# Both half pairs of the first group by halves, with plain fp32 value products for the whole group, in an attention and gated convolution kernel

## The chip, the cores and the metric

One core of one Trainium2 chip runs the whole program. The engines are named as the profile names them: PE (TensorE matmuls), PEld (its weight loads), DVE (VectorE), ACT (ScalarE), POOL (GpSimd) and SP, which here only issues the DMAs. The metric is the device time of one execution in microseconds, lower is better, as the median of repeated executions.

## The reference

Attention within chunks of 64 positions, then a block that gates a projection with a short causal convolution, over 8 batches of 576 positions, 8 heads of 64:

```python
scores = scale * np.matmul(q_c, k_c.transpose(0, 1, 2, 4, 3))      # per chunk of 64 x 64
scores = scores - np.max(scores, axis=-1, keepdims=True)
attn = np.exp(scores)
attn = attn / (np.sum(attn, axis=-1, keepdims=True) + 1e-09)
out = np.matmul(attn, v_c)
# x: (8, 576, 512), the heads side by side
for k in range(5):
    gate_pre += conv_w[k][None, None, :] * xp[:, k:k + S, :]
gate = 1.0 / (1.0 + np.exp(-gate_pre))
val = x @ w_val
return gate * val @ w_out
```

## The kernel before

The 4608 positions are cut into nine groups `g` of 512. In a group the eight heads are two half pairs `p`, and each half pair has two halves `b` of eight blocks of 64 x 64 scores. The channels of x are four chunks `c` of 128, two for each half pair (`c = 2p` and `2p + 1`). All work is written as small pieces, and the string `ORDER` is the program: it lists the pieces one after another, and every engine runs its instructions in the order in which the pieces stand there. `SLOTS` gives each new tile its buffer, in the same order. Nothing is rearranged later, and the waits between engines follow from which piece reads what. All instructions are recorded under one line (L160, the helper `run`), so the rows are read by their tiles.

The pieces of one half pair, in the order in which they need each other: `lq`, `lk`, `lv` (loads of 512 KB), `S g p b` (PE: 16 matmuls 64 x 64, two records each, for one half), `mx` (DVE: row maximum), `sb` (DVE: subtract it), `ex` (ACT: exp), `sm` (DVE: row sum and reciprocal), `nm` (POOL, or `nmD` on DVE: divide), `T` (PE: eight transposes), `ec` (ACT: copy of the transposes out of PSUM), `A` (PE: probabilities times v, giving x), `xc` (ACT: copy of x). `ey` is another way for `sb`, `ex` and `sm`, with a bias and an accumulated sum on ACT.

For the value projection there are two forms. `V g m c` makes three fp32r products for output chunk m and input chunk c (weights v_hi, v_lo, v_hi; x as a rounded part `xr` and a rest `xd`). `F 0 m c` makes one plain fp32 product from the weights before their split (`wq`) and the copied x; the trace records it as two matmuls. The weights arrive as 64 bit numbers, and the pieces `w1` to `w7` put each of the four chunks `v 0` to `v 3` into fp32, on POOL (with a G), DVE and ACT; `w6` and `wb` then split it into v_hi and v_lo.

The other pieces are `k0`, `k` (convolution taps, DVE), `sg` (gate), `gs`, `gr`, `gd` (gate times value, split in two), `P` (output projection, three fp32r products each), `oc`, `st` (copy and store). `W n` makes n matmuls of a zero tile, which nothing reads.

The first group before the change: its two half pairs have one `mx`, `sb`, `ex`, `sm`, `nm`, `T`, `ec`, `A` each, over all sixteen blocks. For half pair (0, 1) the maximum is subtracted by four matmuls on PE (`mh`, `ml`, `sp`, `ep`). `F` serves the chunks c = 0 and 1, `V` the chunks 2 and 3. The opening holds 22 filler matmuls: `W 2` ahead of the first scores, `W 15` after them, then `W 4` and `W 1`.

The set `BY_HALF` names the half pairs that are worked by halves. It is read in `sc`, `half_scores`, `xc`, `x_part`, `xr` and `xd`; before the change it is empty. For a half pair in it, the scores of its second half go to the PSUM tile `et`, and the pieces take a third number, the half.

Of the kernel before, what the change touches and what calls it, by code (L numbers as in the profile page):

```python
# [626 lines left out]
```

## Time and profile before

| | us |
|---|---|
| median of 3 runs | 282.15 (282.10 to 282.59) |
| the profiled execution | 282.13 |
| its span in the trace | 280.3 |
| PE busy in the span | 268.4 |
| DVE busy | 229.7 |
| ACT busy | 208.4 |
| POOL busy | 131.2 |

The span runs from the first to the last instruction of the core; 1.8 us of the execution's own time lie around it. A record of a matmul begins when it starts to stream and ends with its modelled end, so records overlap, and the step from one start to the next tells what one costs.

### The profile page before, as it was taken

How to read it: one execution, taken by the hardware profiler on the slowest of the kernel's cores; microseconds unless marked ns; L12 is line 12 of the kernel's file. 1: busy time of each engine (PE TensorE's matmuls, PEld its weight loads, DVE VectorE, ACT ScalarE, POOL GpSimd, SP SyncE). 2: the span in 40 equal slices, each digit the busy share in tenths (PEclk: the TensorE clock that was granted, in tenths of full speed). 3: DMA queues.
4: the chain of work that ended last, by engine and by line, in shares of the span. 5: the costliest groups of instructions: out<-in, count | busy, mean ns of one | idle time of the engine just before them, and what ended most of it. 6: DMA issues, size and time to landing. Idle time of an engine off the chain costs nothing.

```text
span 280.3 us, 7931 instructions
## 1 busy us (share of the span) xinstructions
PE 268.4 (96%) x3330; PEld 214.4 (76%) x3330; DVE 229.7 (82%) x316; ACT 208.4 (74%) x472; POOL 131.2 (47%) x109
## 2 busy tenths in 40 slices
PE   3979999989999999999999999999999999999994
PEld 2456787867888877888788888888888778888883
DVE  0899999999989999999979998899999676691200
ACT  2477999999899979768796968999687767324331
POOL 1857935093104243991584007379212748642510
PEclk9999999999999999999999999999999999999999
DMA  7999958456002735076442034961104001000526
GB/s 276 417 409 375 322 196 341 125 200 208 0 2 76 268 150 165 24 265 219 160 137 93 1 118 160 317 184 54 40 0 151 4 2 75 0 0 2 187 87 249
DMA packets 14291, 42.47 MB, mean 151 GB/s; under 512 B 1712, under 2 KB 1712, under 8 KB 14256
## 3 DMA queue, kind: packets, MB, share of 16 engines
q1 hardware_dynamic: 14256, 41.97, 41.6%
q8 instruction: 26, 0.43, 0.6%
q14 instruction: 9, 0.07, 0.1%
HBM read 32.53 MB, written 9.44 MB: 150 GB/s over the span
## 4 chain that ended last, share of the span: by engine, by line
PE 89%; DMA 4%; DVE 3%; ACT 1%; issue 1%; POOL 1%; SPq 0%; POOLq 0%
PE ps L160 77%; PE s L160 6%; PE et L160 5%; DMA ld<-in_v 2%; DMA ld<-in_q 1%; DVE rs L160 1%; DVE t L160 1%; DVE mx L160 1%; POOL t L160 1%; ACT t L160 1%; DVE e_row L160 0%; ACT e_row L160 0%; SPq L160 0%; ACT x L160 0%; DVE ml L160 0%
## 5 line engine op out<-in xcount | busy, mean ns | idle before, releaser
L160 DVE SCALAR_TENSOR_TENSOR acc<-x,cw,acc 128x516 f32<-128x516 f32 (+1 forms) x144 | 109.6, 799 | 4.1 <-ACT acc L160 2.3
L160 PE MATMUL ps<-t,v_hi 128*128 128x512 f32 x232 | 81.6, 403 | 0.0
L160 PEld LDWEIGHTS ps<-t,v_hi 128*128 128x128 f32 x232 | 43.6, 188 | 10.5 <-issue 0.5
L160 PE MATMUL ps<-t,v_lo 128*128 128x512 f32 x112 | 44.3, 396 | 0.0
L160 PE MATMUL ps<-o_hi,t 128*128 128x512 f32 x92 | 34.5, 397 | 0.0
L160 DVE TENSOR_REDUCE mx<-s 128x16 f32<-128x1024 f32 x18 | 21.7, 1207 | 7.1 <-PE s L160 7.1
L160 DVE TENSOR_TENSOR t<-ps,t 128x512 fp32r<-128x512 f32 (+1 forms) x27 | 18.0, 683 | 11.1 <-PE ps L160 4.7
L160 PEld LDWEIGHTS s<-ld,ld 64*64 64x64 f32 x1152 | 19.7, 139 | 9.1 <-issue 9.1
L160 PE MATMUL s<-ld,ld 64*64 64x64 f32 x1152 | 22.0, 225 | 4.8 <-DMA ld<-in_q 3.3
L160 PEld LDWEIGHTS ps<-t,v_lo 128*128 128x128 f32 x112 | 21.1, 188 | 5.1 <-issue 0.5
L160 POOL TENSOR_TENSOR t<-e_row,rs 128x1024 f32<-128x1024 f32 x11 | 22.3, 2030 | 1.8 <-DVE cw_h L160 1.1
L160 ACT COPY x<-ps 128x512 f32<-128x512 f32 (+3 forms) x46 | 20.8, 499 | 1.2 <-PE ps L160 1.0
L160 ACT ACTIVATE acc<-x,cw 128x516 f32<-128x516 f32 (+1 forms) x28 | 20.9, 746 | 0.1
L160 PEld LDWEIGHTS ps<-o_hi,t 128*128 128x128 f32 x92 | 17.3, 188 | 4.2
L160 ACT ACTIVATE e_row<-s,mx 128x64 f32<-128x64 f32 x64 | 19.2, 348 | 0.0
L160 PE MATMUL ps<-o_lo,t 128*128 128x512 f32 x48 | 18.9, 394 | 0.0
L160 ACT ACT_TABLE_LOAD x14 | 18.0, 1283 | 1.0 <-PEq L616 0.7
L160 ACT CAST t<-ps 128x512 fp32r<-128x512 f32 x28 | 16.3, 604 | 3.0 <-PE ps L160 3.0
L160 DVE TENSOR_REDUCE rs<-e_row 128x16 f32<-128x1040 f32 x14 | 17.2, 1229 | 0.5 <-ACT e_row L160 0.5
L160 PEld LDWEIGHTS et<-ident,t 128*128 128x128 f32 x128 | 14.6, 141 | 4.0 <-issue 2.1
L160 PE MATMUL et<-ident,t 128*128 128x128 f32 x128 | 16.8, 274 | 0.3 <-DVE t L160 0.3
L160 ACT ACTIVATE e_row<-e_row 128x1024 f32<-128x1024 f32 x13 | 13.9, 1066 | 4.0 <-DVE e_row L160 4.0
(303 smaller groups left out, 609.3 us busy)
## 6 DMA issues: line engine op xcount, KB each, us to landing
ld<-in_k SPq DMA_DIRECT2D x18, 512.0 KB, 5.1
ld<-in_q SPq DMA_DIRECT2D x18, 512.0 KB, 5.9
ld<-in_v SPq DMA_DIRECT2D x18, 512.0 KB, 5.0
out<-t SPq DMA_DIRECT2D x10, 256.0 KB, 4.5
acc<-in_moe_w_val SPq DMA_DIRECT2D x4, 512.0 KB, 7.7
acc<-in_moe_w_out SPq DMA_DIRECT2D x4, 512.0 KB, 5.3
out<-t2h SPq DMA_DIRECT2D x3, 256.0 KB, 2.5
out<-t2g SPq DMA_DIRECT2D x3, 256.0 KB, 2.7
```

The lines of the kernel that those rows point to most:

```text
L160: return tc.keep_in_program_order(fn(*args, **kwargs))
```

## The change

`BY_HALF` holds both half pairs of the first group. Their scores, maxima, exponentials, sums, divisions, transposes, products with v and copies of x are now pieces for one half of eight blocks each (`mx 0 0 0`, `T 0 1 1` and so on). One half of a half pair gives one whole chunk of x (`xc 0 p u` writes chunk `2p + u`). The four maximum matmuls, and `mh`, `ml`, `sp`, `ep`, are not used any more. All sixteen value products of group 0 are `F`; the eight `V 0` pieces (24 fp32r matmuls) and the `xr` and `xd` of half pair (0, 1) are gone. The fillers are four `W 1`. The rest of `ORDER` and `SLOTS` is a new table for the whole program, with some pieces on other engines.

```diff
-ORDER = """zw,zi,zr 0,zr 1,lk 0 0,lq 0 0,W 2,lw v 2,lw v 0,S 0 0 0,zm,S 0 0 1,mx 0 0,w1 v 2,w5 v 2,sb 0 0,lk 0 1,w3G v 2,w2 v 2,
...
+ORDER = """zw,zi,zr 0,zr 1,lk 0 0,lq 0 0,zm,lw v 1,w3G v 1,S 0 0 0,mx 0 0 0,sb 0 0 0,w1G v 1,ex 0 0 0,S 0 0 1,w5 v 1,mx 0 0 1,
+sb 0 0 1,lk 0 1,ex 0 0 1,sm 0 0 0,nmD 0 0 0,T 0 0 0,W 1,lw v 0,w5 v 0,w2 v 1,w1G v 0,lw v 3,w3G v 3,w2 v 0,lv 0 0,
...
 SLOTS = dict(
...
-    et="000000000000000000",
...
+    et="0000000000000000000000",
...
-    mh="0",
-    ml="0",
 )
...
-BY_HALF = set()
+BY_HALF = {(0, 1), (0, 0)}
```

PE, from its first scores on, before (s and et are the scores and transposes, ld a load, ps a product in PSUM, t a probability or weight tile, x the copied x; the fillers between are left out):

```order
L160 MATMUL s_89<-ld_78,ld_80 64x64 x32
...
L160 MATMUL s_167<-ld_130,ld_138 64x64 x32
...
L160 MATMUL et_222<-ident,t_220 128x128 x8
L160 MATMUL s_233<-ld_218,ld_231 64x64 x32
L160 MATMUL ps_287<-t_267,ld_271 64x64
...
L160 MATMUL ps_335<-x_321,t_136 128x512
```

The same place now, up to the scores of the second group's first half pair (s_267):

```order
L158 MATMUL s_87<-ld_78,ld_80 64x64 x16
L158 MATMUL et_110<-ld_78,ld_80 64x64 x16
L158 MATMUL ps_139<-ident,t_137 128x128 x4
...
L158 MATMUL et_164<-t_162,ld_158 64x64 x16
...
L158 MATMUL ps_188<-ident,t_137 128x128 x4
L158 MATMUL s_198<-ld_131,ld_196 64x64 x16
L158 MATMUL et_224<-t_162,ld_158 64x64 x16
L158 MATMUL ps_245<-x_185,t_183 128x512
L158 MATMUL et_247<-ld_131,ld_196 64x64 x16
L158 MATMUL s_267<-ld_222,ld_217 64x64 x32
```

The first value product (ps_335 before, ps_245 now) stood behind three whole sets of scores; it now stands behind three halves, and behind the transposes and products with v of only one half pair.

DVE in the opening, before:

```order
L160 TENSOR_REDUCE mx_123<-s_89 128x16
L160 TENSOR_SCALAR t_125<-acc_85 128x512
L160 TENSOR_TENSOR e_row_64<-s_89,mx_123 128x16x64
L160 SCALAR_TENSOR_TENSOR t_132<-t_125,t_132 128x512
L160 TENSOR_REDUCE rs_141<-e_row_64 128x16
L160 RECIPROCAL rs_141<-rs_141 128x16
L160 TENSOR_REDUCE mx_200<-s_167 128x16
```

DVE in the opening, now:

```order
L158 TENSOR_REDUCE mx_104<-s_87 128x2x4
L158 TENSOR_TENSOR e_row_64<-s_87,mx_104 128x2x4x64
L158 TENSOR_REDUCE mx_104<-et_110 128x2x4
L158 TENSOR_TENSOR e_row_64<-et_110,mx_104 128x2x4x64
L158 TENSOR_REDUCE rs_134<-e_row_64 128x2x4
L158 RECIPROCAL rs_134<-rs_134 128x2x4
L158 TENSOR_TENSOR t_137<-e_row_64,rs_134 128x2x256
```

The weight pieces (t_125, t_132) that stood between maximum and sum have left this stretch, and the division of the first half (t_137) now comes ahead of the second half's sum.

PE at the later value products of group 0, before (v_hi and v_lo are the split weights) and, in the second fence, now:

```order
L160 MATMUL ps_335<-x_321,t_269 128x512
L160 MATMUL ps_357<-x_321,t_269 128x512
L160 MATMUL et_456<-ident,t_445 128x128 x8
L160 MATMUL s_484<-ld_441,ld_452 64x64 x32
L160 MATMUL ps_357<-t_439,v_hi 128x512
L160 MATMUL ps_357<-t_439,v_lo 128x512
L160 MATMUL ps_357<-t_470,v_hi 128x512
```

```order
L158 MATMUL ps_311<-x_185,t2c 128x512
L158 MATMUL ps_311<-x_185,t_155 128x512
L158 MATMUL et_456<-ident,t_445 128x128 x8
L158 MATMUL s_482<-ld_442,ld_471 64x64 x32
L158 MATMUL ps_300<-x_185,t2c 128x512
L158 MATMUL ps_245<-x_185,t2c 128x512
L158 MATMUL ps_245<-x_185,t_155 128x512
```

Where three fp32r products with v_hi, v_lo and v_hi stood for one pair of output and input chunk, one fp32 product (x_185 with t2c or t_155) stands now.

## Rows read from the trace of the kernel before

**Rows 1.** The page: busy time by engine, granted clock, DMA rate, the instruction queue.

```profile
PE 268.4 (96%) x3330; PEld 214.4 (76%) x3330; DVE 229.7 (82%) x316; ACT 208.4 (74%) x472; POOL 131.2 (47%) x109
...
PEclk9999999999999999999999999999999999999999
...
GB/s 276 417 409 375 322 196 341 125 200 208 0 2 76 268 150 165 24 265 219 160 137 93 1 118 160 317 184 54 40 0 151 4 2 75 0 0 2 187 87 249
...
q8 instruction: 26, 0.43, 0.6%
```

**Rows 2.** Windows, five stretches of the span; columns: length, then busy per engine (records).

```profile
0.00:20.30 20.30, 13.73 (x290) 8.53 (x291) 12.44 (x18) 9.46 (x15) 10.42 (x15) 1.00 0.93 366
20.30:30.00 9.70, 9.69 (x220) 6.91 (x221) 9.25 (x15) 7.71 (x14) 7.92 (x6) 1.00 0.98 371
30.00:100.00 70.00, 68.57 (x1024) 55.37 (x1023) 67.62 (x103) 66.55 (x171) 27.42 (x27) 1.00 0.47 164
100.00:200.00 100.00, 99.76 (x1346) 82.00 (x1345) 95.09 (x128) 83.34 (x179) 52.67 (x41) 1.00 0.42 144
200.00:277.00 77.00, 76.66 (x455) 61.59 (x453) 45.27 (x56) 41.04 (x97) 32.76 (x23) 1.00 0.18 68
```

**Rows 3.** Timeline of PE in the opening: start, length, operation [idle before <- releaser].

```profile
5.46 1.99 PE L160 MATMUL s<-ld,ld 64*64 64x64 f32 x64 [3.25 <-DMA ld<-in_q]
7.38 3.88 PE L160 MATMUL ps<-warm 128*128 128x512 bf16 x15
11.36 1.16 PE L160 MATMUL s<-ld,ld 64*64 64x64 f32 x64
...
15.65 1.06 PE L160 MATMUL et<-ident,t 128*128 128x128 f32 x8 [0.31 <-DVE t L160]
...
17.88 1.16 PE L160 MATMUL ps<-t,ld 64*64 64x64 f32 x64
...
20.31 1.10 PE L160 MATMUL ps<-x,t 128*128 128x512 f32 x2 [0.95 <-POOL t L160]
21.24 1.04 PE L160 MATMUL et<-ident,t 128*128 128x128 f32 x8
...
25.09 1.98 PE L160 MATMUL ps<-x,t 128*128 128x512 f32 x4
26.91 1.04 PE L160 MATMUL et<-ident,t 128*128 128x128 f32 x8
```

**Rows 4.** Groups of one shape: busy us, mean ns | idle before; DVE, ACT, POOL.

```profile
L160 DVE TENSOR_REDUCE mx<-s 128x16 f32<-128x1024 f32 x18 | 21.7, 1207 | 7.1 <-PE s L160 7.1
...
L160 ACT ACT_TABLE_LOAD x14 | 18.0, 1283 | 1.0 <-PEq L616 0.7
L160 DVE TENSOR_TENSOR t<-ps,t 128x512 fp32r<-128x512 f32 x26 | 17.3, 682 | 6.4 <-ACT t L160 3.2 <-ACT x L160 3.1
...
L160 DVE TENSOR_REDUCE rs<-e_row 128x16 f32<-128x1040 f32 x14 | 17.2, 1229 | 0.5 <-ACT e_row L160 0.5
...
L160 ACT COPY x<-ps 128x512 f32<-128x512 f32 x22 | 13.0, 601 | 1.1 <-PE ps L160 1.0
...
L160 DVE RECIPROCAL rs<-rs 128x16 f32<-128x16 f32 x18 | 4.6, 253 | 0.6
...
L160 POOL TENSOR_SCALAR t<-acc 128x512 uint32<-128x512 f32 x2 | 4.0, 1996 | 6.1 <-DMA acc<-in_moe_w_val 6.1
...
L160 POOL TENSOR_SCALAR t<-acc 128x512 f32<-128x512 f32 x2 | 1.8, 876 | 0.1
```

**Rows 5.** Timeline of PE, the one gap inside the run, and two fp32r products.

```profile
61.30 0.82 PE L160 MATMUL s<-ld,ld 64*64 64x64 f32 x41
63.55 0.57 PE L160 MATMUL s<-ld,ld 64*64 64x64 f32 x23 [1.43 <-issue]
...
74.10 0.40 PE L160 MATMUL ps<-o_hi,t 128*128 128x512 f32 x1
74.33 0.39 PE L160 MATMUL ps<-o_lo,t 128*128 128x512 f32 x1
```

More of the change, by code (lines that the diff above doesn't have):

```diff
@@ new lines @@
+w4 v 1,w7G v 1,w2 v 3,lk 1 0,A 0 0 1,xc 0 0 1,mx 0 1 0,sb 0 1 0,F 0 1 0,S 0 1 1,w5 v 3,ex 0 1 0,S 1 0 0,S 1 0 1,F 0 3 0,
+w4 v 3,lc,mx 0 1 1,sb 0 1 1,F 0 3 1,w3 c 0,ex 0 1 1,F 0 2 0,sm 0 1 0,w7G v 3,nm 0 1 0,T 0 1 0,w1 c 0,lw v 2,lw o 0,
+w1G v 2,mx 1 0,w5 v 2,w1G o 0,F 0 1 1,lq 1 1,F 0 2 1,sm 0 1 1,nm 0 1 1,ec 0 1 0,w2 c 0,lv 0 1,A 0 1 0,sb 1 0,w2 v 2,
+w3 v 2,w3 o 0,ex 1 0,w4 v 2,w5 c 0,xc 0 1 0,sm 1 0,hl 0,w7G v 2,T 0 1 1,ec 0 1 1,lk 1 1,S 1 1 0,S 1 1 1,A 0 1 1,
+xc 0 1 1,lk 2 0,F 0 2 2,nm 1 0,mx 1 1,sb 1 1,F 0 2 3,w6 v 3,w6 v 2,wb v 2,w6 v 0,w4 c 0,T 1 0,lw o 3,w5 o 3,w3 o 3,
@@ new lines @@
+hl 1,xd 1 1 0,T 2 0,ec 2 0,lq 4 0,V 1 2 0,k0 0 2,k 0 3 1,k 0 2 1,k 0 1 3,k 0 3 2,ea 3 0,V 1 3 0,V 1 2 1,lw o 1,w3 o 1,
+w1G o 1,V 1 3 1,V 1 3 2,k 0 3 3,k 0 2 2,k 0 1 4,lq 3 1,lv 2 1,lv 2 0,V 1 1 0,V 1 1 1,V 1 1 2,V 1 1 3,V 1 3 3,vc 1 3,
+k 0 3 4,vc 1 1,k 0 2 3,sg 0 3,sg 0 1,k 0 0 4,sg 0 0,V 1 2 2,V 1 2 3,A 2 0,xr 2 0 0,xr 2 0 1,k 0 2 4,lk 3 1,gsG 0 3,
+S 3 1 0,S 3 1 1,mx 3 1,T 2 1,ec 2 1,w2 o 1,rc 3 0,w1G o 2,V 1 0 0,V 1 0 1,xc 2 0 1,xc 2 0 0,w4 o 3,sb 3 1,V 1 0 2,
+V 1 0 3,vcD 1 2,vc 1 0,S 4 0 0,xd 2 0 0,w5 o 1,gs 0 1,gsG 0 0,xd 2 0 1,k0 1 3,w3 o 2,S 4 0 1,A 2 1,xr 2 1 1,xd 2 1 1,
@@ new lines @@
+vc 4 1,lk 8 1,k 4 3 1,gd 3 1,st 1 2,st 1 3,k 5 3 2,V 4 2 2,k 4 1 2,V 4 2 3,st 1 1,lv 6 1,lv 6 0,ec 6 0,lq 7 1,k0D 5 1,
+vc 4 2,k 5 1 1,k 5 1 2,k 5 1 3,sm 6 1,V 5 3 0,V 5 3 1,V 5 3 2,V 5 3 3,P 3 1 0,P 3 1 1,k 5 3 3,V 5 0 0,k 4 1 3,nmD 6 1,
+k 4 1 4,k 5 3 4,k 5 1 4,gd 3 3,ea 7 0,vc 5 3,P 3 1 2,V 5 0 1,P 3 0 0,V 5 0 2,V 5 0 3,vc 5 0,P 3 0 1,P 3 0 2,P 3 0 3,
+k 4 0 1,k 4 0 2,V 5 1 0,rc 7 0,k 4 3 2,oc 3 0,sg 5 3,V 4 0 0,V 4 0 1,V 4 0 2,V 4 0 3,vc 4 0,sg 4 1,P 3 3 0,P 3 3 1,
+P 3 3 2,P 3 3 3,k 4 3 3,oc 3 3,k 4 0 3,P 3 1 3,oc 3 1,T 6 1,sg 4 2,A 6 0,k 4 0 4,sg 4 0,gsG 4 0,k 4 3 4,xc 6 0 1,
@@ new lines @@
+xr 6 0 0,xcD 6 0 0,S 7 1 0,S 7 1 1,V 5 1 1,sg 4 3,xd 6 0 0,lq 8 1,xr 6 0 1,gr 4 0,ec 6 1,mx 7 1,st 3 3,lv 7 1,st 1 0,
+P 3 2 0,P 3 2 1,P 3 2 2,P 3 2 3,hl 6,k0 6 1,xd 6 0 1,sb 7 1,ocD 3 2,gs 4 3,ex 7 1,sm 7 1,nm 7 0,T 7 0,gd 4 0,k0 6 0,
+A 6 1,xr 6 1 1,gsG 4 1,xc 6 1 1,xc 6 1 0,xr 6 1 0,xd 6 1 0,sg 5 1,S 8 1 0,S 8 1 1,xd 6 1 1,V 5 1 2,gs 5 3,k0G 5 0,
+k 5 0 1,k 5 0 2,V 5 2 0,k0 6 2,V 5 1 3,V 5 2 1,V 5 2 2,k 5 2 1,k 5 2 2,ec 7 0,gr 5 3,V 6 0 0,V 6 0 1,V 6 0 2,V 6 0 3,
+vc 6 0,gdD 5 3,k 5 0 3,gm 5 1,k 5 2 3,V 6 1 0,k 5 2 4,k 5 0 4,k 6 2 1,lv 7 0,gr 4 1,V 6 1 1,V 6 1 2,V 6 1 3,st 2 3,
@@ new lines @@
+xd 8 0 0,gsG 6 1,gsG 6 2,xr 8 0 1,oc 5 3,hl 8,gsG 6 0,lv 8 1,P 5 2 0,P 5 2 1,P 5 2 2,st 4 2,xc 8 0 0,sg 7 0,P 5 2 3,
+oc 5 2,gr 6 1,xd 8 0 1,A 8 1,xc 8 1 1,xcD 8 0 1,k 7 1 4,V 7 3 0,xr 8 1 0,gd 6 1,xd 8 1 0,xr 8 1 1,V 7 3 1,V 7 1 0,
+xd 8 1 1,V 7 3 2,V 7 3 3,xc 8 1 0,k0 8 0,gsG 7 0,gr 6 0,gd 6 0,sg 7 2,gsG 7 2,gr 7 2,st 4 3,V 8 2 0,V 8 2 1,V 8 2 2,
+V 8 2 3,k0G 7 3,gr 6 2,gd 6 2,k 8 0 1,k 8 0 2,k 8 0 3,V 7 1 1,V 7 1 2,st 3 0,gs 6 3,sg 7 1,gr 7 0,gd 7 0,gr 6 3,gd 6 3,
+V 8 0 0,k 8 0 4,sg 8 0,vcD 7 3,k0 8 3,V 8 0 1,V 8 0 2,V 8 0 3,gm 8 0,vc 8 2,V 8 1 0,V 7 1 3,gr 8 0,k0 8 2,P 6 2 0,
@@ L106 @@
+    t2="0123456789abcdefghijklmnopqrs4312789a6c05bhjrg4mdkseao0i198lf6nh3cgbj4mds0297ilq6gp8f0e1jir256b4qnh3"
+       "8cm91koi0ejrlf63gbms7h25p1dij0851jf6egrlk0m43p8on9bic2sge46d1790jbp4c45fmqn8ogepd93n2s1ji0qhrklm8bpe"
+       "176codg45banrh6jg2s935bp0q6nm81je245",
+    t4="0123456789ab0123456a72b890147356ab2089147532b6145a089160a2b173624589",
     x="010101010",
```

136 lines of the change are left out of this document (53 added, 83 removed).

## The prediction

> **What bounds the kernel now.** I first read the busy times of the page and then the windows, to see which engine never rests. PE is busy 268.4 of 280.3 us [rows 1]. By stage: before 20.3 us it is busy 13.7 of 20.3 us, and from there to its last matmul it is idle about 2 us in all, of which 1.43 us are a single gap [rows 2, 5]. So from 20.3 us on the end is set by PE's own list of work, whatever the other engines do, as long as they stay ahead. DVE and ACT have little room up to about 100 us (67.6 and 66.6 us busy of 70) and much after 200 us [rows 2]. Two things can therefore move the end: how long PE's list is, and how early PE may begin to work through it without a pause.
>
> The timeline of PE shows the opening [rows 3]. The first scores start at 5.46 us, when k and q have landed. They are followed by fifteen fillers, the second scores, fillers and the four maximum matmuls; the first transposes come at 15.65, the first product with v at 17.88 and the first value product at 20.31 us, after a wait of 0.95 us for POOL. In these 20 us PE does useful work worth some 5 us: three scores, one set of transposes, one product with v.
>
> [...]
>
> **The list gets longer.** Eight fp32 products replace eight triples of fp32r products. Two fp32 products (four records) start at 25.09 and the next operation at 26.91 us [rows 3]: 0.91 us each, with a change of operation in it; I take 0.88. An fp32r product steps 0.233 us (74.10 to 74.33) [rows 5], a triple 0.70. So 8 x 0.88 - 24 x 0.233 = 7.0 - 5.6 = +1.4 us. Halved transposes and halved products with v keep their total work and add some changes of operation; I put 0.2 us on those behind the opening, an estimate. The maximum matmuls and the fillers ran ahead of 20.3 us, where the end is not set, so taking them out saves nothing by itself.
>
> **The list begins earlier.** I walk the new opening with row durations. Half a step has 512 elements: 0.68 us on DVE out of PSUM and 0.60 on ACT; full reductions take 1.21 and 1.23 us, so I take 0.68 for half of either, and 0.25 for a reciprocal [rows 4]. PE's two halves of scores, at the low level, end at 6.46 and 7.46 us (5.46 + 1.99 in two parts). DVE: maximum 6.5 to 7.2, subtract to 7.9, the second half's maximum and subtract to 9.2, the first half's sum and reciprocal to 10.0, its division to 10.8. ACT's exp of the first half (7.9 to 8.5) is hidden under DVE. PE's four transposes then take about 1.1 us at the low level (eight took 1.06 at the full one) and end at 11.9. ACT has weight steps queued ahead of its copy: the last waits for three steps of POOL (2.0 + 0.88 + 0.88 us from the landing of the weights at about 7.4) and ends near 11.9 too, so the copy ends at 12.5. v is the seventh load of 0.52 MB: 276 GB/s for the first slice of 7 us and 417 after it [rows 1] bring 3.7 MB by about 11.2 us, so it is there. The first half's product with v runs 12.6 to 13.7 (half of 1.16 us, doubled for the low level). After a filler the second half's transposes end near 15.1, the half score S 0 1 0 at 16.1, the second product with v, now at the full level, at 16.7; the first value product ends at 17.5, S 0 1 1 at 18.0 and S 1 0 at 19.0 us.
>
> At that point PE has done what it had done at 20.31 us before, plus one value product (20.31 to 21.24 [rows 3]). So the lead is 21.2 - 19.0 = 2.2 us.
>
> Is the lead kept? The next pieces on PE are scores, fp32 products and transposes worth 8 us up to A 0 1 1, the product with v of the second half of half pair (0, 1). What it waits for runs on DVE and ACT behind S 0 1 1: maximum, subtract, the sums of both halves, a whole maximum and subtract of half pair (1, 0), then on ACT its exp and two copies. By the same durations that is 8 us too; I charge 0.1 us of waiting. DVE and ACT lose the rests and casts of half pair (0, 1) and gain half steps. By the instructions that come and go in the whole program, at such durations, DVE's work grows by about 1 us, and ACT's falls by about as much although two more table loads (1.28 us each [rows 4]) stand in it (estimates); the room after 200 us covers both. Loads keep their number and size. I see no place where the later order must stall, and give that 0 here and a case below.
>
> **The sum.** +1.4 +0.2 +0.1 -2.2 = -0.5 us. Against the profiled execution's 282.13 us (its span of 280.3 and 1.8 around it), which stands within 0.02 us of the median of 282.15, that is 281.6 us.
>
> Its largest unknown is the level of PE's clock in the opening, since nothing in the trace shows PE with so little work there. From above: all of the new opening at full level. Then transposes, products with v and half scores cost half, the same walk reaches S 1 0 at 17.3 us, the lead is 3.9 and the time 279.9. From below: the low level up to the end of S 1 0. Then the value product takes 0.9 us more, S 0 1 1 0.5 and S 1 0 1.0 more, S 1 0 ends at 21.4 and the time is 284.0. I take the value between, because PE is at work nearly without pause from 12.6 us on, and in the rows the level had changed within the first scores and fifteen fillers (5.46 to 11.3 us) [rows 3].
>
> [...]
>
> **Rivals.** (a) *The gap goes.* PE stands 1.43 us in the middle of one half pair's scores at 62.1 us, and nothing that the profile shows is waited for (issue) [rows 5]. The instruction queue moved 26 packets [rows 1], and PE's 2 x 3330 records are 26 times 256 (6660 to 6656). I read the gap as one late packet of instructions. The new list places the packets elsewhere. One of 26 was late, so none, one or two late ones are all likely. With none, 281.6 - 1.4 = 280.2 us.
>
> [...]
>
> (b) *The clock stays low*, at one place: from A 0 0 0 to the end of S 0 1 1. Its price is the value product at twice its time (0.9 us) and half a score (0.5): the lead falls to 0.8 us and the time is 283.0, slower than before. It decides once the low level lasts beyond the first value product, at about 17 us. For it speaks that PE rests from 7.5 to 10.8 us and works only in short pieces up to 12.6; against it, that it is then dense for some 5 us.
>
> (c) *A later wait takes the place of the lead.* Between 30 and 100 us DVE and ACT are busy 97 and 95 of 100 [rows 2]. The first group's half steps, the two table loads, or a second late packet of instructions can make PE wait there: one event of 1.4 us gives 283.0.
>
> (d) *It doesn't do what it says:* POOL's weight steps or the seventh load are later than I put them, the first value product starts no earlier than 17.2 us, and the lead of 1.7 pays just for the longer list: 282.1.
>
> **How the numbers follow.** What can be told from no change here is about 0.2%, 0.56 us. The forecast, 281.6 (281.0 to 282.2 with the terms' small errors): 0.38, of which 0.23 beyond 0.2% faster and 0.15 within. (a) 280.2: 0.22, of which 0.21 faster. (b) 283.0: 0.19, of which 0.15 slower and 0.04 within. (c) 283.0: 0.17, of which 0.14 slower and 0.03 within. (d): 0.04, within. Sums: faster 0.44, same 0.27, slower 0.29. The range runs from 279.8, a little below (a) and at the full level's bound, to 283.3, which takes in most of (b) and (c) and leaves out their upper ends; about 2 in 10 lie outside.
>
> **What would show it.** In the changed kernel's PE timeline: the first value product near 16.7 us, and S 1 0 ended near 19.0 us; the half scores and half products with v at 0.5 us (full level) or 1.0 us (low); fp32 products at 0.88 us; no idle PE after that but one gap of issue or none. If S 1 0 ends after 20.5 us, the step on the clock or on the loads was wrong; if it ends near 19 and the time is still over 282.5, the lead was given back, and the windows will show in which stretch PE was idle.

## The result and the profile after

The change made the kernel 1.2% slower, with an interval that lies above 1, and the prediction (281.6 us) was wrong in sign.

| | before | changed |
|---|---|---|
| median of the runs | 282.1 us | 285.9 us |
| ratio to before, 95% interval | | 1.0119 [1.0071, 1.0167] |
| the same program a second time (e1), ten runs | 281.9 us | 284.8 us, 1.0087 [1.0054, 1.012] |
| profiled execution, its span | 282.13, 280.3 us | 284.93, 283.1 us |

(Some executions were disturbed: the ratios leave them out, the medians don't, and the profiles of e4 and e14 are of such executions, so that only waits are read from the second.)

The page of the changed kernel, busy time of the engines and shares of the chain of waits; the busy times of before are in [rows 1], and the chain of before is in the second fence:

```profile
PE 266.6 (94%) x3298; PEld 212.2 (75%) x3300; DVE 235.1 (83%) x326; ACT 208.1 (73%) x469; POOL 132.8 (47%) x113
...
PE 82%; ACT 7%; DVE 7%; DMA 2%; issue 1%; SPq 0%; ACTq 0%
```

```profile
PE 89%; DMA 4%; DVE 3%; ACT 1%; issue 1%; POOL 1%; SPq 0%; POOLq 0%
```

PE's records fell from 3330 to 3298 and its share from 96 to 94%. ACT and DVE are now 14% of the chain that ended last (4% before). The windows answer to [rows 2] (length, then busy time and records of PE, weight loads, DVE, ACT, POOL, then clock, DMA share and GB/s):

```profile
30.00:100.00 70.00, 68.70 (x1015) 53.25 (x1015) 69.34 (x103) 67.18 (x167) 34.57 (x29) 1.00 0.51 181
100.00:200.00 100.00, 100.00 (x1404) 82.04 (x1403) 94.23 (x128) 84.85 (x175) 46.23 (x38) 1.00 0.39 131
```

From 30 to 100 us PE is idle 1.30 us (1.43 before), from 100 to 200 us not at all. So the loss is not plain idle time that could be read off one window. It lies in the first 101 us: S 5 0 has the same number of scores, value products and output products ahead of it in both orders, and it starts at 101.39 us instead of 98.64, 2.75 us later, while the whole span is 2.8 us longer. The timeline of PE in the opening answers to [rows 3]:

```profile
6.11 1.13 PE L158 MATMUL s<-ld,ld 64*64 64x64 f32 x32 [6.11 <-DMA ld<-in_q]
...
11.75 1.09 PE L158 MATMUL ps<-ident,t 128*128 128x128 f32 x4 [3.65 <-DVE t L158]
13.51 1.13 PE L158 MATMUL et<-t,ld 64*64 64x64 f32 x32 [0.67 <-ACT t L158]
...
14.98 0.91 PE L158 MATMUL ps<-ident,t 128*128 128x128 f32 x4
15.81 0.69 PE L158 MATMUL s<-ld,ld 64*64 64x64 f32 x32
...
17.18 1.13 PE L158 MATMUL ps<-x,t 128*128 128x512 f32 x2
...
18.76 0.45 PE L158 MATMUL s<-ld,ld 64*64 64x64 f32 x17
20.19 0.92 PE L158 MATMUL s<-ld,ld 64*64 64x64 f32 x47 [0.99 <-issue]
21.05 2.84 PE L158 MATMUL ps<-x,t 128*128 128x512 f32 x6
23.73 0.60 PE L158 MATMUL ps<-ident,t 128*128 128x128 f32 x4
```

The reader is to see four things. The first scores start at 6.11 us, 0.65 later than before. The opening runs at the low clock (32 scores in 1.13, four transposes in 1.09 us) until about 15 us and at the full one from S 0 1 0 on (32 in 0.69). This is read from durations, and the trace's own list of clock changes agrees: its first entry, 1.00, is at 15.60 us here and at 8.36 us in the kernel before. Ahead of the first entry the trace has no value, and the views print 1.00 there; so the 1.00 in the opening, which [rows 2] has too, is no reading of the clock. The first value product starts at 17.18 us, not far from the 16.7 of the prediction. And inside S 1 0 PE stands for 0.99 us with nothing to wait for (issue), so that S 1 0 is done at 21.05 us instead of 19.0. The 2.2 us of lead have become 21.24 - 21.05 = 0.2 us.

Behind the opening, the places where PE waits (before had one, the 1.43 us of [rows 5], and 0.24 us at 135 us):

```profile
62.68 0.50 PE L158 MATMUL ps<-t,v_hi 128*128 128x512 f32 x1
63.02 0.39 PE L158 MATMUL ps<-t,v_lo 128*128 128x512 f32 x1
64.15 0.96 PE L158 MATMUL ps<-t,v_hi 128*128 128x512 f32 x2 [0.74 <-DVE t L158]
64.95 0.39 PE L158 MATMUL ps<-t,v_lo 128*128 128x512 f32 x1
...
77.63 0.40 PE L158 MATMUL ps<-o_hi,t2b 128*128 128x512 f32 x1
78.31 0.50 PE L158 MATMUL ps<-o_lo,t2b 128*128 128x512 f32 x1 [0.28 <-DVE o_lo L158]
...
92.76 0.85 PE L158 MATMUL ps<-t,ld 64*64 64x64 f32 x41 [0.22 <-issue]
```

The first three rows are one triple of V 2 0 0: its third record comes 1.13 us after the second, where 0.23 is usual.

### The profile page after: what moved, and what is told of

It reads as the page before. It is cut to its first block, busy times and chain, and to the rows that moved or that the text cites. A ratio compares the mean times of both kernels' runs of the same rounds, so it can differ in the third digit from the quotient of the medians.

```text
span 283.1 us, 7872 instructions
## 1 busy us (share of the span) xinstructions
PE 266.6 (94%) x3298; PEld 212.2 (75%) x3300; DVE 235.1 (83%) x326; ACT 208.1 (73%) x469; POOL 132.8 (47%) x113
## 4 chain that ended last, share of the span: by engine, by line
PE 82%; ACT 7%; DVE 7%; DMA 2%; issue 1%; SPq 0%; ACTq 0%
PE ps L158 71%; PE et L158 5%; PE s L158 5%; DVE t L158 2%; ACT t L158 2%; ACT e_row L158 2%; DMA ld<-in_q 2%; DVE acc L158 1%; DVE rs L158 1%; ACT x L158 1%; DVE mx L158 1%; ACT L158 0%; DVE t4a L158 0%; DVE o_lo L158 0%; DVE e_row L158 0%
## 5 line engine op out<-in xcount | busy, mean ns | idle before, releaser
L158 DVE SCALAR_TENSOR_TENSOR acc<-x,cw,acc 128x516 f32<-128x516 f32 (+1 forms) x144 | 113.6, 825 | 1.7 <-POOL t2n L158 0.7
L158 PE MATMUL ps<-t,v_hi 128*128 128x512 f32 x216 | 75.2, 402 | 0.8 <-DVE t L158 0.7
L158 PEld LDWEIGHTS ps<-t,v_hi 128*128 128x128 f32 x216 | 40.6, 188 | 11.2 <-DVE t L158 1.7
L158 ACT COPY t<-ps 128x512 f32<-128x512 f32 x29 | 16.7, 585 | 25.6 <-PE ps L158 25.6
L158 POOL TENSOR_TENSOR t<-e_row,rs 128x1024 f32<-128x1024 f32 (+1 forms) x12 | 23.4, 1954 | 13.7 <-DVE rs L158 12.2
L158 DVE TENSOR_REDUCE mx<-s 128x16 f32<-128x1024 f32 (+1 forms) x18 | 20.7, 1153 | 7.8 <-PE s L158 7.7
L158 ACT ACTIVATE e_row<-e_row 128x1024 f32<-128x1024 f32 (+1 forms) x16 | 15.3, 955 | 9.8 <-DVE e_row L158 9.6
L158 ACT ACT_TABLE_LOAD x16 | 20.5, 1283 | 1.0 <-PEq L614 0.7
L158 ACT COPY x<-ps 128x512 f32<-128x512 f32 (+3 forms) x36 | 15.4, 469 | 3.9 <-PE ps L158 2.2
L158 DVE TENSOR_TENSOR t<-ps,t 128x512 fp32r<-128x512 f32 x22 | 14.6, 684 | 4.2 <-ACT t L158 3.9
L158 POOL TENSOR_TENSOR t<-t,t 128x512 f32<-128x512 f32 (+2 forms) x6 | 8.1, 1358 | 21.1 <-ACT t L158 17.7
L158 DVE TENSOR_REDUCE rs<-e_row 128x16 f32<-128x1040 f32 (+1 forms) x16 | 17.5, 1092 | 0.3 <-ACT e_row L158 0.3
```

The costliest lines, as they stand in the source:

```text
L158: return tc.keep_in_program_order(fn(*args, **kwargs))
```

## Experiments

The figures of this table are from the timelines of PE. "S 1 0 done" is the start of the next operation behind it; "v late" is PE's wait for the load of v at the product A 1 1, between 41 and 46 us; "64 us" is its wait for DVE inside V 2 0 0.

| kernel | first scores | gap in S 1 0 | S 1 0 done | v late | 64 us | span |
|---|---|---|---|---|---|---|
| changed | 6.11 | 0.99 | 21.05 | 0 | 0.74 | 283.1 |
| e1 the same again | 5.47 | 0.3 | 19.72 | 0 | 0.73 | 281.6 |
| e3 eight fillers | 6.21 | 2.35 | 21.92 | 0 | 0.72 | 285.9 |
| e6 70 short fillers | 5.36 | 0 | 21.46 | 0.63 | 0.72 | 287.2 |
| e7 DVE's order | 5.42 | 1.29 | 21.07 | 1.20 | 0 | 285.1 |
| e8 e6 and e7 | 5.49 | 0 | 18.93 | 0 | 0 | 289.0 |
| e9 less work on DVE | 5.39 | 0.3 | 19.89 | 1.28 | 0.74 | 282.9 |
| e10 products ahead of S 1 0 | 5.96 | 0 | 21.57 | 0.84 | 0.73 | 287.5 |
| e11 50 short fillers | 5.60 | 0 | 20.58 | 1.49 | 0.73 | 283.4 |
| e12 place of v | 5.35 | 0.3 | 19.72 | 0 | 0.73 | 282.0 |
| e13 and first v | 5.40 | 1.36 | 21.00 | 0 | 0.73 | 283.0 |
| e15 and 50 short fillers | 5.42 | 0 | 20.72 | 0 | 0.73 | 283.8 |

(A gap of 0.3 is no row of its own: 64 scores take 1.40 to 1.46 us there instead of 1.16. In e10 two value products of 0.9 us have been done by then that the others do behind S 1 0.)

### e1: the same program again

> The changed kernel once more, unaltered. In its first profile the first scores started at 6.11 us (5.46 before), PE stood 0.99 us for nothing that the profile shows (issue) inside S 1 0, and waited for DVE at 64.2 and 78.3 us. If these are properties of the program they come back within 0.1 us and the time is 285.2; if the first load and the gap are chance, S 1 0 ends up to 1.6 us earlier than 21.05 us and the time is down to 283.6.

```profile
5.47 1.14 PE L158 MATMUL s<-ld,ld 64*64 64x64 f32 x32 [5.47 <-DMA ld<-in_q]
...
18.35 1.44 PE L158 MATMUL s<-ld,ld 64*64 64x64 f32 x64
19.72 2.84 PE L158 MATMUL ps<-x,t 128*128 128x512 f32 x6
...
62.82 0.50 PE L158 MATMUL ps<-t,v_hi 128*128 128x512 f32 x1 [0.73 <-DVE t L158]
```

284.8 us in the median of ten, between the two forecasts. The two losses of the opening are in part chance: this execution started its first scores at 5.47 us and lost 0.3 instead of 0.99 us inside S 1 0. S 1 0 was done 1.33 us earlier, and the span is 1.5 us shorter. So PE's list does set the end, and what the opening gains arrives there. The wait at 62.8 (64.2 in the first profile) keeps its size to 0.01 us: it moves with the opening, and is a property of the program.

### e2: the list by itself

```diff
-V 0 2 2,V 0 3 2,V 0 2 3, ... V 0 3 3, ... V 0 1 2, ... V 0 1 3, ... V 0 0 2,V 0 0 3
+F 0 2 2,F 0 3 2,F 0 2 3, ... F 0 3 3, ... F 0 1 2, ... F 0 1 3, ... F 0 0 2,F 0 0 3
```

> The kernel before with one thing of the change alone: its eight triples of fp32r value products of the first group (V 0 m 2 and V 0 m 3) are single fp32 products (F), at the same places; the casts and rests of half pair (0, 1) are still made, though nothing reads them. Theory that PE's list sets the end: the time grows by the price of the products; my sum had 8 x 0.88 - 24 x 0.233 = +1.4 us (283.5), the changed kernel's own steps of 0.905 us give +1.65 (283.8). Theory that DVE and ACT set PE's pace between 30 and 80 us: a longer list of PE there is hidden in part, under +0.8 us (282.9 or less).

283.4 us against 281.9, ratio 1.0046 [1.0016, 1.0075]: +0.5 to +2.1 us, in the middle +1.3. The middle is the price of the products, and not the under +0.8 of the theory that PE's longer list is hidden in part; the lower end of the interval doesn't quite exclude that theory. In the changed kernel's own opening three products in a row step 2.68 us (21.05 to 23.73), 0.89 each, and 0.905 where each ends in a change of operation; 8 x 0.905 - 24 x 0.233 = 1.65.

### e3, e6, e8, e11: fillers in the opening, for the clock and the packets

e3:

```diff
-S 0 0 1,w5 v 1, ... T 0 0 0,W 1,lw v 0
+S 0 0 1,W 8,w5 v 1, ... T 0 0 0,lw v 0
```

> The changed kernel with the first of its one-matmul fillers (W 1) made eight and put right behind the second half's scores, where PE rests from 8.1 to 11.75 us. If the low clock of the opening is what took the lead, transposes and products with v take half, the first value product starts near 15.8 instead of 17.18 us, S 1 0 ends near 19.7 and the time is 1.3 us under that of the changed kernel (283.9). Theory that DVE and ACT set the pace from 28 to 78 us: S 1 0 ends earlier as well, but PE waits longer at 64 and 78 us and the time is within 0.4 us of the changed kernel's (284.8 to 285.6).

```profile
8.13 3.23 PE L160 MATMUL ps<-warm 128*128 128x512 bf16 x8
12.23 0.63 PE L160 MATMUL ps<-ident,t 128*128 128x128 f32 x4 [0.87 <-DVE t L160]
13.54 0.69 PE L160 MATMUL et<-t,ld 64*64 64x64 f32 x32 [0.68 <-ACT t L160]
...
17.86 0.39 PE L160 MATMUL s<-ld,ld 64*64 64x64 f32 x10
20.60 1.39 PE L160 MATMUL s<-ld,ld 64*64 64x64 f32 x54 [2.35 <-issue]
21.92 4.11 PE L160 MATMUL ps<-x,t 128*128 128x512 f32 x6
```

The clock did rise (four transposes in 0.63, the product with v in 0.69), and the first value product started at 16.29 us though the first load was late. But the gap in S 1 0 grew to 2.35 us, and the three products behind it took 4.11 us instead of 2.84. Windows of the stretch show why (columns as above, the clock is the first number behind POOL):

```profile
17.00:20.60 3.60, 1.26 (x43) 0.77 (x42) 3.42 (x8) 2.15 (x5) 1.83 (x3) 1.00 1.02 405
21.20:24.40 3.20, 3.20 (x33) 1.77 (x26) 2.33 (x4) 0.00 (x0) 1.79 (x4) 0.50 1.04 413
24.60:28.00 3.40, 3.40 (x12) 1.52 (x10) 1.59 (x4) 1.49 (x4) 0.75 (x2) 1.00 0.76 307
```

After the pause the granted clock is 0.50 for the next products. 285.5 us, 1.0103 [1.0027, 1.0178]: what the clock gave, the gap took.

e6 (a new piece, matmuls of 64 x 64 columns of the same bf16 tile):

```diff
-S 0 0 1,w5 v 1, ... T 0 0 0,W 1,lw v 0
+S 0 0 1,Y 70,w5 v 1, ... T 0 0 0,lw v 0
```

> The changed kernel with its first filler replaced by 70 short ones (64 columns each) right behind the second half's scores, where PE rests from 7.4 to 11.2 us. They are 140 more instructions of PE ahead of the opening's dense part, so the packet that was needed inside S 1 0 is asked for some 3 us earlier. If the gap in S 1 0 (0.99, 0.28 and 2.35 us in three profiles) is a packet of instructions that waits behind the opening's loads, it is gone (under 0.1 us) and the executions lie closer together, near the lowest of the changed kernel: 283.4. If the short fillers also raise the clock earlier, transposes and products with v take half and it is 282.9. If gap and clock don't count because DVE sets the pace, the time stays at 284.8.

> The changed kernel with the 70 short fillers of the opening and the two moves on DVE together. If the opening's gap and DVE's order are separate losses on one path they add up: 281.6 to 282.4, level with the kernel before (281.9), since its list is still some 1.5 us longer and the lead of the opening pays for that. If they overlap, it is no better than the better one of the two alone.

289.0 us, 1.0235 [1.0194, 1.0276], and 290.5 us, 1.0295 [1.0242, 1.0348]. The gap in S 1 0 was gone in both, as expected, but both times were missed by far. e8 (e6 with the two moves of e7) is the one profile with the opening of the prediction:

```profile
17.89 1.11 PE L160 MATMUL s<-ld,ld 64*64 64x64 f32 x64
18.93 2.84 PE L160 MATMUL ps<-x,t 128*128 128x512 f32 x6
...
28.74 0.34 PE L160 MATMUL et<-t,ld 64*64 64x64 f32 x8 [2.00 <-issue]
```

S 1 0 is done at 18.93 us (19.0 was predicted). Ten microseconds on PE stands for 2.00 us inside the next run of small matmuls (A 0 1 0, T 0 1 1, S 1 1, A 0 1 1), and the clock reads 0.50 from 29.2 to 32.4 us. 140 more instructions have moved the place at which a packet is used up into another dense run. In e6 v came 3.24 us late for A 0 0 0, and a gap of 1.29 us followed at 30.6 us, in the same dense run as e8's. Further on both kernels have a gap of issue that the changed kernel has not, at 183 to 185 us (1.52 us in e6, 1.25 in e8), and e8 one of 0.96 us at 152 us.

e11 (50 short fillers, and a product between the small matmuls of that run):

```diff
-F 0 1 1, ... F 0 2 1, ... A 0 1 0, ... T 0 1 1
+F 0 1 1, ... A 0 1 0,F 0 2 1, ... T 0 1 1
```

> The changed kernel with 50 short fillers (100 instructions) in the opening's rest and the value product F 0 2 1 between the product with v A 0 1 0 and the transposes T 0 1 1, so that no 256 instructions of PE in a row are short matmuls from the point at which a packet is used up. With 70 fillers S 1 0 ended at 18.93 us when v was there in time, but gaps of 1.3 and 2.0 us came at 28 to 30 us and the clock fell after them. Theory of the late packet: S 1 0 ends at 18.9 to 19.5 us, no gap up to 30 us is over 0.5 us, the clock does not fall again, and the time is 1 to 2 us under the changed kernel's (282.8 to 283.8). If fillers cost by themselves, whatever the packets do, the time is again 286 or more.

285.6 us, 1.0126 [1.0072, 1.0181]. No gap was left up to 44 us, so the packets behave as expected; but v was late twice (2.10 us at A 0 0 0, 1.49 at A 1 1), and behind the first of them the clock was low again (0.50 from 14.4 to 17.6 us). The time was missed.

### e4, e10: products ahead of S 1 0

```diff
-S 0 1 1,w5 v 3,ex 0 1 0,S 1 0 0,S 1 0 1,F 0 3 0, ... F 0 3 1
+S 0 1 1,w5 v 3,ex 0 1 0,F 0 3 0,F 0 3 1,S 1 0 0,S 1 0 1, ...
```

> The changed kernel with two ready value products (F 0 3 0 and F 0 3 1) put ahead of S 1 0 instead of behind it and behind the last subtract of half pair (0, 1), so that PE uses up its instructions more slowly between 17.7 and 20.2 us. If the 0.99 us of issue inside S 1 0 is a packet of instructions that comes too late for 64 short matmuls in a row, the gap is gone or under 0.3 us and, if PE's list alone sets the end, the time is 1.0 us less (284.2). If DVE and ACT set the pace up to 78 us, S 1 0 comes 0.8 us later for DVE and the time stays (285.2) or grows by up to 0.8 us (286.0).

> The changed kernel once more with F 0 3 0 and F 0 3 1 ahead of S 1 0 (its first profile fell into a disturbed execution and shows nothing). If the gap in S 1 0 is a late packet, 1.8 us of value products after the second quarter of the dense stretch leave time for it: a gap of 0 to 0.3 us there instead of 0.28 to 1.3. The time by its nine earlier executions is level with the changed kernel's (median 284.6 against 284.8), so that what is won there has to be lost again: I expect DVE to be short of work for up to 0.8 us at 19 to 22 us, since S 1 0 ends 1.8 us later for it, and PE to wait by as much at 64 us.

285.3 us (1.0099 [1.006, 1.0139]) and, on another chip, 289.5 us (1.0286 [1.0251, 1.0321]). In the second profile S 1 0 runs through in 1.16 us with no gap, and at T 0 1 0, behind the products that both have done by then, PE stands 0.14 us behind e1 (22.54 against 22.40), as it did at the first value product (0.11). So the gap was bought off at no price, and nothing was won over e1 either, whose gap was 0.3. The 289.5 us come from elsewhere: v late by 0.84 us, and a gap of 2.27 us inside S 7 0 at 147 us with the low clock behind it (0.50 from 148.3 to 151.5 us). I did not expect that one; e10's other runs on this chip lie as high (289.2 to 290.7), and why is open. So the expected wait of 0.8 us at 64 us was wrong as well (0.73, as ever).

### e5: the gap of the kernel before

```diff
-V 2 3 0,hl 2,w7G o 3,lq 5 1,lk 4 0,V 2 3 1,A 2 1
+A 2 1,V 2 3 0,hl 2,w7G o 3,lq 5 1,lk 4 0,V 2 3 1
```

> The kernel before with one PE step moved: the product with v of half pair (2, 1) (A 2 1) stands ahead of the value products V 2 3 0 and V 2 3 1 instead of behind them, so that A 2 1 and the scores S 4 0 are no longer 128 short matmuls (with their weight loads 256 instructions) in a row. If the 1.43 us of issue inside S 4 0 are a packet of instructions that comes too late for such a row, the gap is gone or under 0.3 us and the time is 1.1 to 1.4 us under that of the kernel before (about 280.7). If the gap has another cause, it stays near 1.4 us, there or at the same time of the run, and the time is unchanged (281.9).

```profile
60.74 1.32 PE L160 MATMUL ps<-t,ld 64*64 64x64 f32 x64
61.99 0.50 PE L160 MATMUL ps<-t,v_hi 128*128 128x512 f32 x1
...
63.59 0.91 PE L160 MATMUL s<-ld,ld 64*64 64x64 f32 x42
64.69 0.57 PE L160 MATMUL s<-ld,ld 64*64 64x64 f32 x22 [0.19 <-issue]
```

The 1.43 us [rows 5] have become 0.19: two triples between the 64 small matmuls of A 2 1 and those of S 4 0 are enough. By this pair the gap goes with a run of some 256 instructions of PE that passes in 2 us. The count of PE's instructions, at the end of this document, shows it more directly. The time hardly moved: 281.9 against 282.2 us, 0.9992 [0.9972, 1.0012]. The profile's first scores came at 6.32 us and its first value product 1.8 us later than in the profile of before; from there to the end it was 1.0 us shorter. In e2, which has the same list of scores, the gap was 0.69 us, so 1.43 was a bad case and not the usual one.

### e7, e9, e14: the waits for DVE

e7:

```diff
-xd 2 0 0,w5 o 1,gs 0 1,gsG 0 0,xd 2 0 1
+xd 2 0 0,w5 o 1,gsG 0 0,xd 2 0 1,gs 0 1
...
-wbD o 3,sm 3 1,w6 o 1,W 1,wbD o 1
+wbD o 3,w6 o 1,wbD o 1,sm 3 1,W 1
```

> The changed kernel with two steps of DVE moved: the gate product gs 0 1 (1.80 us there, 0.69 elsewhere, while POOL works) stands behind the rest xd 2 0 1 that V 2 0 0 waits for instead of ahead of it, and the weight rest wbD o 1 that P 0 2 1 waits for (with its cast w6 o 1 on ACT) ahead of the sums sm 3 1. If DVE's order there makes PE wait at 64.2 (0.74 us) and 78.3 us (0.28 us), both waits are gone, and with PE's restart behind each the time is 1.0 to 1.9 us less than the changed kernel's 284.8. If DVE's whole load sets the pace, the waits appear at the next products and the time is within 0.4 us of 284.8.

```profile
44.10 1.16 PE L160 MATMUL ps<-t4a,ld 64*64 64x64 f32 x64 [1.20 <-DMA ld<-in_v]
...
67.80 0.50 PE L160 MATMUL ps<-t4a,v_hi 128*128 128x512 f32 x1 [0.34 <-DVE t4a L160]
...
79.05 0.50 PE L160 MATMUL ps<-o_lo,t2b 128*128 128x512 f32 x1 [0.38 <-DVE o_lo L160]
...
81.67 0.50 PE L160 MATMUL ps<-o_hi,t2m 128*128 128x512 f32 x1 [0.71 <-DVE t2m L160]
```

286.1 us, 1.0127 [1.0077, 1.0177]. The wait at 64 us is gone, and V 2 0 1 comes 0.9 us earlier against the opening than in e1. Others came (0.34 and 0.71, and 0.26 at 98.8 us), the one at 78 us grew from 0.28 to 0.38, and v was late.

e9:

```diff
-k 0 1 4, ... k 0 3 4, ... k 0 0 4, ... k 0 2 4
```

> The changed kernel with the last of the five convolution taps of the first group left out on its four channel blocks (k 0 0 4 to k 0 3 4): four steps of DVE at 0.68 us each, 2.7 us, between 50 and 58 us. Nothing else is changed. If the load of DVE from 28 to 78 us is what makes PE wait for it (0.74 us at 64.2, 0.28 at 78.3 in the changed kernel; moved to 67.8, 79.1, 81.7 and 98.8 us when DVE's order was changed), both waits are gone, no other takes their place up to 100 us, and the time is 1.0 to 1.6 us under the changed kernel's 284.8 (283.2 to 283.8). If the waits come from ACT's own queue or from single steps held up by POOL, they stay and the time changes by less than 0.4 us.

Here the last tap of the first group's convolution is not computed. DVE's timeline, then a row of PE:

```profile
56.65 1.23 DVE L160 TENSOR_REDUCE mx<-s 128x16 f32<-128x1024 f32 x1 [2.79 <-PE s L160]
...
61.00 0.69 DVE L160 TENSOR_TENSOR t<-ps,t 128x512 fp32r<-128x512 f32 x1 [0.23 <-ACT x L160]
61.61 1.80 DVE L160 TENSOR_TENSOR t<-t2k,t2s 128x512 f32<-128x512 f32 x1
63.33 0.68 DVE L160 TENSOR_TENSOR t<-ps,t 128x512 fp32r<-128x512 f32 x1
```

```profile
64.06 0.96 PE L160 MATMUL ps<-t,v_hi 128*128 128x512 f32 x2 [0.74 <-DVE t L160]
```

284.7 us in the profiled execution, and a ratio of 1.0164 [1.0085, 1.0243] that rests on two runs: not the 283.2 to 283.8 of the theory, but v was late by 1.28 us. Against e1, which had nearly the same opening and v in time, the span is 1.3 us longer: what v took, and nothing won. DVE now rests 2.79 us, until the scores S 3 1 are there, and the wait at 64 us is still 0.74 us. So the theory that DVE's load makes PE wait has fallen for this wait. From the end of S 3 1 DVE has a row of steps in its queue (maximum, a reciprocal, a weight step, subtract, a copy, xd 2 0 0, the gate product gs 0 1) ahead of xd 2 0 1, for which V 2 0 0 waits; it ends at 64.0 whether DVE was rested or not. It is the order on DVE, tied to PE's own scores, and gs 0 1 in it takes 1.80 us.

e14 (as e13 below, with the first of e7's two moves):

> As e13, with DVE's gate product gs 0 1 behind the rest xd 2 0 1. The wait of 0.73 us at 64 us (0.72 to 0.74 in seven profiles) should go, as in e7, where V 2 0 1 came 0.9 us earlier against the opening. If that wait is a loss of its own, the time is 0.7 to 1.0 us under e13's; if the next waits (67.8, 79.1, 81.7 us in e7) stand in the same loop of DVE and ACT, they take it back and the time is within 0.3 us of e13's.

284.8 us, 1.0094 [1.0075, 1.0113], against e13's 1.0128 [1.0107, 1.0148]: about 0.3% less, 0.4 to 0.9 us. The wait at 64 us is gone and looks like a loss of its own, though the two intervals touch; 0.37 us at 68 and 0.66 at 79.5 us took some of it back.

### e12, e13: the place of a load

In the changed kernel lv 1 1, the v of half pair (1, 1), stands behind lk 4 0 and has the ring place of lv 1 0, which PE reads up to 37 us. The queue of loads, of the changed kernel and of before:

```profile
37.48 0.33 SPq L158 DMA_DIRECT2D ld<-in_v  x1
```

```profile
29.10 0.33 SPq L160 DMA_DIRECT2D ld<-in_v  x1
```

It is issued at 37.48 us for a product at 42.8, against 29.10 for 40.3 before. Where PE had to wait for it, it landed 6 to 7 us after its issue (in e9 issued at 36.35, there at 43.0). In nine profiles of the changed order v was late in five, by 0.6 to 1.5 us.

```diff
-lk 4 0,lq 3 0,w5 o 2,lk 3 0,lv 1 1
+lv 1 1,lq 3 0,w5 o 2,lk 3 0,lk 4 0
...
-    ld="012345013240512304512504024135302415034035501523524103",
+    ld="012345013240512304512304024153502413054053301325324105",
```

> The changed kernel with the loads lv 1 1 and lk 4 0 exchanged, in the queue and in the ring of load buffers (the later users of the two places exchanged with them, so all else is as it was). lv 1 1 then takes a place that is free at 27.3 us and is issued near 31.3 instead of 36 to 37.5 us; lk 4 0 is not needed before 59 us. If the late issue of this load is what makes PE wait at 41 to 44 us in some executions, that wait is gone in the profile, and the executions come down to the best ones of the changed kernel: median 283.4 to 283.9 instead of 284.8 to 285.9. If loads are late by chance wherever they stand, the median stays within 0.4 us of 284.8.

```profile
31.33 0.42 SPq L160 DMA_DIRECT2D ld<-in_v  x1
```

284.1 us, 1.0076 [1.0058, 1.0095]. The load is issued 5 to 6 us earlier, and no profile with this exchange (e12 to e15) shows the wait. In time it is 0.7 us below e1's median, with intervals that overlap; five of the six runs lie between 283.6 and 284.7, near the forecast of 283.4 to 283.9 but not all within it.

e13:

```diff
-lw v 3,w3G v 3,w2 v 0,lv 0 0
+lv 0 0,lw v 3,w3G v 3,w2 v 0
```

> As e12, and the first load of v (lv 0 0) one place earlier in the queue, ahead of the weights lw v 3, so that it lands some 1.2 us earlier than at 12.3 to 12.9 us. At the opening's low clock the first product with v starts at 12.9 to 13.5 us for the copy of ACT, not for v, so I expect no gain over e12 beyond 0.2 us (283.4 to 283.9); a gain of 0.5 us or more would say that v was the later of the two in most executions.

285.3 us, 1.0128 [1.0107, 1.0148]: slower than e12, which I had not expected. The profiles differ in one place, the gap in S 1 0 (1.36 against 0.3 us), and from there PE is 1.3 us later, 1.0 at the end. The packet of instructions for that place began at 17.56 us instead of 16.55. The intervals of e12 and e13 don't overlap, which speaks against chance; how the earlier v would make the packet later stays open.

### e15: the opening once more

As e13, with e11's two changes.

> As e13, with the 50 short fillers in the opening's rest and F 0 2 1 between A 0 1 0 and T 0 1 1 (as in e11). With v in time the clock, which rose at 10.9 us in e11 and fell again during the 2.1 us wait for v, should stay at the full level: first product with v at 12.5 to 13.0 us, S 1 0 ended at 18.6 to 19.2 us (19.0 in the prediction), no gap in it. If the opening's lead is paid in full once loads and packets are in time, the time is 1.0 us under e13's: 282.4 to 282.9, still above the kernel before by the longer list less the lead. If PE's later waits swallow it, it is level with e13.

284.3 us, 1.0089 [1.0069, 1.0109]. There was no gap, but v was 0.82 us late at 13.4 us although it was loaded earlier, the opening ran at the low clock up to 18 us (a half score in 1.13 us, a half product with v in 1.10), and S 1 0 was done at 20.72 instead of 18.6 to 19.2 us. The time is 0.9 us under e13's, about the forecast difference, but not by the forecast way. In three kernels with short fillers the clock was up early (e6, e8, e11: the first transposes in 0.63 us) and in this one it wasn't (1.09); the opening of the prediction came about in one of them only.

No version beats the kernel before. The best of the changed order is e12, 0.8% above it; the kernel before with its gap closed (e5) is level with it.

## Why the prediction was wrong

**What bounds the kernel: right.** The end follows PE's list: e1 and the first profile differ by 1.33 us at S 1 0 and by 1.5 at the end, e12 and e13 by 1.28 and 1.0.

**The sum.** In the profiled pair the span grew by 2.8 us. Its terms, as forecast and as measured:

| term | forecast | measured |
|---|---|---|
| eight fp32 products for 24 fp32r | +1.4 | +1.65 by the steps; e2 +1.3 (0.5 to 2.1) |
| halves, changes of operation | +0.2 | +0.3 |
| later waits, new less old | +0.1 | +0.3 |
| lead of the opening | -2.2 | -0.2 (-1.5 in e1 and e12) |
| not placed | | +0.7 |

The third line: 64 us costs 1.24 us with what PE loses in taking up again (2.27 from 62.68 to 64.95 for what takes 1.03 at 41.34 us in the kernel before), 78 us 0.56, 92.8 us 0.5; before, 61.30 to the end of S 4 0 cost 1.7 and 135 us 0.3. The second: T 0 1 and A 0 1 whole took 0.87 and 1.04 us, their halves 0.43, 0.59, 0.62 and 0.58. The last is what is left over, and where it lies is not shown.

Of the 3.3 us between forecast and measurement 2.0 are the lead and 1.3 the other lines. The lead alone didn't decide the sign: with a lead of 1.5 us (e1, e12) the span was still 1.3 and 1.6 us longer than before, so by these two the full 2.2 us would have left the kernel 0.6 to 0.9 us slower, an estimate.

**The list: right mechanism, size off by 0.25 us.** I took 0.88 for an fp32 product from two in a row; with the changes of operation around them it is 0.905.

**The lead: the step that failed.** "So the lead is 21.2 - 19.0 = 2.2 us" held in e8 alone (18.93); the first profile had 0.2 us, e1 and e12 1.5. Three things stood in its way. The first load: I kept 5.46 us from before, and the executions start at 5.35 to 6.3 us, both kernels (5.46, 5.52 and 6.32 with the order of before). DVE's steps: the first transposes came at 11.2 us in e1, e7, e12 and e13, whose load was in time, not at 10.8. The first maximum began 1.19 us after the scores did where I had 1.04, a step that needs the one before it began 0.72 us after it and not 0.68, and the division took 0.77 us in e1 and 0.88 in e12. And the packet: I had the mechanism, in rival (a), and used it only for the one gap in the trace of before. The new opening puts the product with v, scores and transposes behind each other where before they stood between fillers and waits. PE gets through some 115 small matmuls and their weight loads between 15.8 and 19.2 us, and the next packet is late by 0.3 to 1.4 us (2.35 where the fillers of e3 made it denser still). So the walk, which added up PE's own steps, was too short by what PE's instructions need to arrive.

**The clock: right.** What the prediction calls the low and the full level are the two paces of [rows 3], 64 scores in 1.99 and in 1.16 us. Its walk takes the one as half the other; for the small pieces no run shows a factor of two: half scores took 1.13 us against 0.69 and four transposes 1.09 against 0.63, 1.6 and 1.7 times as long. A value product did take about twice its time: 1.83 us from start to start in e8, with the granted clock at 0.50, against 0.89. I took the low level up to the half score S 0 1 0 and the full one from the product behind it on. In the first profile S 0 1 0 is already at full (0.69), in e7 still low (1.13): right to one piece. Rival (b) didn't happen. Rival (d) stands at its edge (first value product at 17.18, in e1 at 16.78 us), but what followed was not its case. My last sentence, that an S 1 0 ended after 20.5 us would mean a wrong step on the clock or the loads, was too narrow: 0.65 us were the load, 0.99 the packet.

**"I see no place where the later order must stall": failed.** Such places are there, as rival (c) had it: v of A 1 1 at 41 to 44 us in five profiles of nine, and DVE at 64 and 78 us. They didn't eat the lead of the first profile, which was lost before 21 us; there they cost 0.3 us more than the waits of before. The diff showed both places. One of SP's queue: the new ring gave lv 1 1 a place that is free only at 36 to 37 us, and I said that loads keep their number and size and did not look when each is issued. One of DVE's queue: gs 0 1 stands between the two rests of half pair (2, 0), where before they stood together. I had the high load of DVE and ACT (97 and 95 of 100) as the reason for such a wait, and for the one at 64 us that was wrong too: with 2.7 us less of work on DVE it was the same (e9). DVE's work grew by 5.4 us (229.7 to 235.1) and not by about 1; 4.0 of it are the 144 convolution taps (113.6 against 109.6 us), as many as before.

**Rival (a), the gap goes:** it did go from 62 us, and came back in S 1 0. Its price of 1.43 us was a bad case; 0.69 in e2.

## What to carry to other kernels

PE ran out of instructions here where small ones follow each other densely (some 115 matmuls and their weight loads in 3.4 us): count where a new order puts its dense runs, and keep long operations between them (two triples took the gap of the kernel before from 1.43 to 0.19 us). Fillers shift the count, and with it every later place (140 instructions more, and the gap at 20 us stood at 29 to 31). When an order moves, list for every load when its buffer comes free and when it is needed; a count of loads says nothing. And a gap or a landing read from one profile is one draw: two profiles of the same program differed by 1.5 us here, more than half of the change's whole effect.
